# A list scheduler's rules re-tuned on a fused attention-and-MLP kernel: which step goes next, what is loaded first

## The chip, the cores and the metric

The kernel runs on one core of one Trainium2 chip. The metric is device time in microseconds of one execution, lower is better. The kernel before takes 282.93 us (median of 6 runs, 282.83 to 283.55). Ratios are computed from the mean time of one kernel's fast runs over the mean of the other's fast runs of the same rounds, so they are not quite the ratio of the medians that are quoted.

Engine names: PE is the matrix engine, DVE the vector engine, ACT the scalar engine, POOL the general one, SP the queue that issues all DMAs here.

## The reference, cut to what matters

x is 2048 tokens of 640 features in bf16. It is layer-normed once to xn, and two branches are added to it:

```python
def _A_ref(x, wqkv, w_phi, wo):        # 32 heads of 20
    q, k, v = split(x @ wqkv)
    pq, pk = q @ w_phi, k @ w_phi      # per head
    phi_q = concat(softmax(pq), softmax(-pq)); phi_k = concat(softmax(pk), softmax(-pk))
    kv = phi_k^T @ v;  z = sum over tokens of phi_k
    return (phi_q @ kv) / (phi_q @ z + 1e-6) merged @ wo
def _B_ref(x, w1, w3, w2):             # 1536 wide
    return (silu(x @ w1) * (x @ w3)) @ w2
xn = layernorm(x)
return x + _A_ref(xn, ...) + _B_ref(xn, ...)
```

Linear attention: the key side of all 2048 tokens has to be summed before the first query can be finished. The MLP has no such barrier, so its steps can fill holes in the attention branch.

## The kernel before

The program is not written in the order in which it runs. Eight generators ("streams") each offer their next step. A step is a short group of instructions. A loop asks every stream for its head, estimates with a cost table when that step could start, commits the best one to the instruction lists, and goes on. The result is a fixed list for every engine, and the engine works through it in that order: where PE's next matmul waits for a DMA, PE stands still (0.9 us before the fold in the profile below).

```python
streams = [norms(), attention(), k_norms(), loads(), fold_k(), o_transposes(), mlps(), outs()]
while any(alive):
    best = None
    for i in range(n):
        ...                                     # head of stream i, recorded as ops
        if any(o.eng == "PE" for o in ops):
            at = max(P.ready(ops), P.free["PE"] + 0.15)
        else:
            at = P.start_of(ops[0])
            if i == 2 and at < P.free["PE"] + 3.0:
                at -= 4.0                       # key sums early
            if i == 0 and at < P.free["PE"] + 2.0:
                at = -1.0                       # norms first of all
        if best is None or at < best[0]:
            best = (at, i, ops, after)
    ...
    P.commit(ops)

def first_loads():
    load_x(0, 1)
    load_x(1, 2)
    P.dma("SP", phi_s[:], phi_t)
    P.dma("SP", wv[:], wqkv_t[:, :, 2 * D:3 * D])
    load_x(2, 4)
    P.dma("SP", wqkT[:, DC:2 * DC, :], A_wqkv[:, D:2 * D], True)   # key weights, transposed by the DMA
    load_x(4, 8)
    w13(0, 512)                                                    # first third of w1 and w3, 1.31 MB
    load_x(8, 12)

def loads():                                    # cut: later transfers, after x tiles are normed
    for t in range(4, T):
        ...
        yield lambda t=t: P.dma("SP", xnT[:, :, t * 128:(t + 1) * 128], x_tok[:, t, :], True)
        if t == 7:
            yield lambda: (w13(512, 1024), load_x(12, 16))
        if t == 9:
            yield lambda: w13(1024, 1536)
            yield lambda: P.dma("SP", wqkT[:, 0:DC, :], A_wqkv[:, 0:D], True)   # query weights
```

The steps that the text speaks of: an *eviction* copies a result of PE out of its bank, by DVE or ACT, so that the bank is free again; the *warm-up* matmuls work on zeros before any data is there; a *value tile* or *key tile* is 10 matmuls of 320 columns for 128 tokens; the *fold* multiplies the transposed key weights (tile wqkT) with the block-diagonal of w_phi (tile BDc) into Wkp, which every key tile needs; a *q tile* is the last attention step of 128 tokens, with a chain of six DVE instructions behind it (the 1.5 us one writes prod); an *MLP step* is 10 matmuls of 512 columns and two DVE instructions (tiles t and hT); an *output tile* is 34 matmuls of 320 columns and one DVE add.

The softmax here doesn't subtract the row's maximum and nothing guards it: scores larger than these inputs give would overflow.

Of the kernel before, what the change touches and what calls it, by code (L numbers as in the profile page):

```python
# [9 lines left out]
D = 640  # L10
# [3 lines left out]
T = S // 128  # L14
# [228 lines left out]
def bass_parallel_sum__linear_kernel_hedgehog__glu_gated_swiglu__prompt_kernel(  # L243
# [13 lines left out]
    P = _Program(nc)  # L257
# [47 lines left out]
    wv = new("wv", [128, DC, D], bf, RKV + 6400)  # L305
# [87 lines left out]
    wqkv_t = A_wqkv.rearrange("(c p) n -> p c n", p=128)  # L393
# [4 lines left out]
    def w13(a, b):  # L398
        P.dma("SP", w1_s[:, :, a:b], w1_t[:, :, a:b])
        P.dma("SP", w3_s[:, :, a:b], w3_t[:, :, a:b])  # L400

    def load_x(a, b):
        P.dma("SP", x_tok[:, a:b, :], x_t[:, a:b, :])

    def first_loads():
        load_x(0, 1)
        load_x(1, 2)
        P.dma("SP", phi_s[:], phi_t)
        P.dma("SP", wv[:], wqkv_t[:, :, 2 * D:3 * D])
        load_x(2, 4)  # L410
        P.dma("SP", wqkT[:, DC:2 * DC, :], A_wqkv[:, D:2 * D], True)
        load_x(4, 8)
        w13(0, 512)
        load_x(8, 12)


# [29 lines left out]
    def ln_apply(t):  # L446
        o, m, s, z = x_tok[:, t, :], mv[:, t, 0:1], rstd[:, t, 0:1], rstd[:, t, 1:2]
        if t < 4 or P.free["DVE"] < P.free["ACT"]:
            P.op("DVE", "tensor_scalar", [o], [o, m, s], (o, o, m, s, ALU.subtract, ALU.mult),
                 cost=0.45)  # L450
        else:
            P.op("ACT", "activation", [o], [o, s, z], (o, o, ACT.Identity), dict(bias=z, scale=s),
                 cost=0.9)
# [138 lines left out]
    def load_xres(t):  # L592
        P.dma("SP", xres[:, t % 4, :], x_t[:, t, :])
# [30 lines left out]
    done = dict.fromkeys(("w", "ln", "t", "f", "k", "n", "kv", "q", "o", "h"), 0)  # L624

    def norms():
        yield lambda: (first_loads(), consts())
        for t in range(4):
            yield lambda t=t: ln_stats(t, 1)
            if t % 2:  # L630
                yield lambda t=t: ln_apply(t - 1)
                done["ln"] = t
                yield lambda t=t: ln_apply(t)
                done["ln"] = t + 1
            if t == 1:
                yield block_diag
        todo = []
        for t in range(4, T + 2, 2):
            if t == T or t > done["k"] + 6:
                for u in todo:  # L640
                    yield lambda u=u: ln_apply(u)
                    done["ln"] = u + 1
                todo = []
            if t == T:
                break
            while t > done["k"] + 6:
                yield None
            yield lambda t=t: ln_stats(t, 2)
            for u in todo:
                yield lambda u=u: ln_apply(u)  # L650
                done["ln"] = u + 1
            todo = [t, t + 1]
        yield consts_late

    def fold_k():
        for dc in range(DC):
            yield lambda dc=dc: fold_mm(1, dc, banks(2))
        done["f"] += 1
# [3 lines left out]
    def k_norms():  # L662
        for t in range(T):
            while done["k"] <= t:
                yield None
            yield lambda t=t: k_norm(t)
            done["n"] = t + 1

    def transposed(t):
        while done["ln"] <= t:  # L670
            yield None
        yield lambda: xn_transpose(t, banks(1))
        done["t"] = t + 1

    def loads():
        while done["t"] < 4:
            yield None
        for t in range(4, T):
            while done["ln"] <= t:
                yield None  # L680
            yield lambda t=t: P.dma("SP", xnT[:, :, t * 128:(t + 1) * 128], x_tok[:, t, :], True)
            done["t"] = t + 1
            if t == 7:
                yield lambda: (w13(512, 1024), load_x(12, 16))
                done["w"] = 8
            if t == 9:
                yield lambda: w13(1024, 1536)
                done["w"] = 12
                yield lambda: P.dma("SP", wqkT[:, 0:DC, :], A_wqkv[:, 0:D], True)
                done["f"] = 2  # L690

    def attention():
        def v(t):
            return lambda: v_tile(t, banks(2))

        yield lambda: warm_up(10, True)
        yield from transposed(0)
        yield lambda: warm_up(4, False)
        yield from transposed(1)
        yield v(0)  # L700
        yield v(1)
        yield from transposed(2)
        yield from transposed(3)
        yield v(2)
        yield v(3)
        while done["f"] < 1:
            yield None
        for t in range(T):
            while done["t"] <= t:
                yield None  # L710
            yield lambda t=t: k_tile(t, banks(2))
            done["k"] = t + 1
            if t >= 4:
                yield v(t)
            if 9 <= t < 14:
                while done["f"] < 2:
                    yield None
                yield lambda dc=t - 9: fold_mm(0, dc, banks(2))
        yield lambda: P.dma("SP", wo_s[:], A_wo.rearrange("(c p) d -> p c d", p=128))
        for fc in range(DC):  # L720
            yield lambda fc=fc: q_proj(0, fc, banks(1))
        while done["n"] < T:
            yield None
        for fc in range(DC):
            for sg in range(2):
                yield lambda fc=fc, sg=sg: kv_sum(sg, fc, banks(1))
        done["kv"] = 1
        yield lambda: P.dma("SP", w2_s[:], B_w2.rearrange("(c p) d -> p c d", p=128))
        yield lambda: (load_xres(0), load_xres(1))
        for b in range(NB):  # L730
            for j in range(4):
                t = 4 * b + j
                yield lambda t=t: q_tok(t, banks(4))
                done["q"] = t + 1
                if b + 1 < NB:
                    for fc in range((5 * j + 3) // 4, (5 * j + 8) // 4):
                        yield lambda b=b, fc=fc: q_proj(b + 1, fc, banks(1))

    def o_transposes():
        for t in range(T):  # L740
            while done["q"] <= t:
                yield None
            yield lambda t=t: P.dma("SP", oT[:, :, t * 128:(t + 1) * 128], o_tok[:, t % 3, :], True)
            done["o"] = t + 1

    def mlps():
        for b in range(NB):
            for fc in range(FC):
                while done["t"] < 4 * b + 4 or done["w"] <= fc or b == 2 and done["t"] < T or b == 3 and not done["kv"]:
                    yield None  # L750
                yield lambda b=b, fc=fc: mlp(b, fc, banks(2))
            done["h"] = b + 1

    def outs():
        for t in range(T):
            while done["o"] <= t or done["h"] <= t // 4:
                yield None
            yield lambda t=t: out_tile(t, banks(2))

    streams = [norms(), attention(), k_norms(), loads(), fold_k(), o_transposes(), mlps(), outs()]  # L760
    n = len(streams)
    heads, alive = [None] * n, [True] * n
    while any(alive):
        best = None
        for i in range(n):
            if heads[i] is None and alive[i]:
                s = next(streams[i], StopIteration)
                if s is StopIteration:
                    alive[i] = False
                else:  # L770
                    heads[i] = s
            if heads[i] is None:
                continue
            save = nmlp[0], len(finish)
            ops = P.step(heads[i])
            after = nmlp[0], finish[save[1]:]
            nmlp[0] = save[0]
            del finish[save[1]:]
            if any(o.eng == "PE" for o in ops):
                at = max(P.ready(ops), P.free["PE"] + 0.15)  # L780
            else:
                at = P.start_of(ops[0])
                if i == 2 and at < P.free["PE"] + 3.0:
                    at -= 4.0
                if i == 0 and at < P.free["PE"] + 2.0:
                    at = -1.0
            if best is None or at < best[0]:
                best = (at, i, ops, after)
        if best is None:
            continue  # L790
        at, i, ops, after = best
        nmlp[0] = after[0]
        finish.extend(after[1])
        P.commit(ops)
        heads[i] = None
# [61 lines left out]
```

## Time and profile before

| what | before |
|---|---|
| time, median of 6 | 282.93 us |
| span in the profile | 281.4 us |
| PE busy in it | 275.2 us (98%) |
| usual spacing of starts, 512 columns / 320 columns | 216 / 136 ns |
| sum of usual spacings over all 1890 matmuls | 271.7 us, 3.0 us of it warm-up |

The page of the kernel before: its first line of busy times, and three rows in which each digit is the busy share of one fortieth of the span in tenths (PEclk is the granted clock of PE).

```profile
PE 275.2 (98%) x1890; PEld 168.6 (60%) x1890; DVE 180.6 (64%) x317; ACT 108.6 (39%) x194; POOL 59.3 (21%) x90
...
PE   7799999999999999999999999999999999999996
...
DVE  4477988998464689989989999996631212121212
...
PEclk9999999999999999999999999999999999999999
```

PE is full almost everywhere, at full clock. What can still be won are small waits. The list of waits of PE (who waits, what ended the wait by the profile, us in total, times, longest; it counts no idle time under 150 ns):

```profile
PE PS L101 <- DVE t_68 L101: 1.6, 2, 1.3
PE PS L101 <- DMA wqkT<-in_A_wqkv_dram: 0.9, 1, 0.9
PE PS L101 <- DMA wv<-in_A_wqkv_dram: 0.5, 1, 0.5
PE PS L101 <- ACT Wkp L101: 0.5, 1, 0.5
```

The 1.3 us of the first line are the time before the first warm-up matmul. This list is not the whole loss. A matmul's end in the profile is its latency, not its turn on the array: the Trainium skill, "TensorE: Matmul & The Clock Gate", Single matmul latency, gives (398 + N) / 2.4 ns, that is 379 ns at 512 columns, and Back-to-back issue gap gives N / 2.4 + 2.5 for the gap of an isolated matmul, that is 216 ns; this trace has 379 ns, and 216 ns in unbroken streams. So a wait under 163 ns (379 - 216) leaves no idle time at all in the profile, and a longer one shows 163 ns too little. Below, "lost" is therefore the spacing between the starts of two neighbouring matmuls less the usual (median) spacing of that shape.

The timeline of PE in the kernel before, late in the attention stage (start, duration, what, idle before):

```profile
178.83 0.81 PE L101 MATMUL PS<-xnT,w_s 128*128 128x512 bf16 x3
179.72 0.86 PE L101 MATMUL PS<-KVc,EqT_81 128*128 128x154 bf16 x12
180.84 0.82 PE L101 MATMUL PS<-xnT,w_s 128*128 128x512 bf16 x3 [0.26 <-DVE t_68 L101]
```

Three 512-column matmuls need 0.65 us, and 0.89 us lie between the first two starts: 0.24 us lost, with no idle time listed (what is left of it, 0.08 us, is under 150 ns). Twelve q-tile matmuls need 0.69 us and took 1.12: 0.42 lost, where the profile lists 0.26. A third such place at 184.96 us costs 0.25 us. The busy table by stretches of the same kernel (window, its length, then busy us and instruction counts of PE, PE's weight loads, DVE, ACT, POOL; then clock, DMA share, GB/s) says why:

```profile
165.00:180.00 15.00, 14.92 (x95) 7.54 (x93) 14.30 (x27) 5.27 (x12) 0.00 (x0) 1.00 0.12 22
180.00:195.00 15.00, 14.65 (x76) 6.66 (x74) 13.32 (x23) 4.15 (x8) 0.00 (x0) 1.00 0.20 34
```

DVE is as full as PE there, and with q tiles and MLP steps alternating it falls behind.

The chain of waits of the kernel before (start, us, what), its start and one place of its later part:

```profile
3.33 8.43 DMA wqkT<-in_A_wqkv_dram
...
11.89 0.49 PE PS L101 x6
...
13.70 0.61 ACT Wkp L101
...
14.35 150.95 PE PS L101 x1062
...
178.17 1.50 DVE prod L101
...
180.11 0.69 DVE t_68 L101
```

At the start the transposed key weights (wqkT, landed at 11.76 us) and an eviction of the fold bound PE; from 165 to 185 us DVE pieces stand in the chain.

### The profile page before, as it was taken

To read this page: it belongs to the slowest core of one execution; us is meant where nothing else is said; L and a number is where in the kernel's file an instruction comes from. 1 tells how busy PE (TensorE), PEld (TensorE's weight loads), DVE (VectorE), ACT (ScalarE), POOL (GpSimd) and SP (SyncE) were. 2 spreads that over 40 slices of the span, in tenths; PEclk is the share of its full clock that TensorE was granted. 3 is DMA by queue.
4 is the path that set the end of the run, shared out by engine and by line. 5 is a ranking of instruction groups with operands and counts; after the bars stand their busy time and mean duration, and the time that the engine had idled before them with its cause. 6 is when DMAs were issued, how large, how long until landed. Compare 5 with 4: busy or idle time off the path is not lost.

```text
span 281.4 us, 4619 instructions
## 1 busy us (share of the span) xinstructions
PE 275.2 (98%) x1890; PEld 168.6 (60%) x1890; DVE 180.6 (64%) x317; ACT 108.6 (39%) x194; POOL 59.3 (21%) x90
## 2 busy tenths in 40 slices
PE   7799999999999999999999999999999999999996
PEld 2567765775469555555555555444467777777774
DVE  4477988998464689989989999996631212121212
ACT  3589888888510454474454533322200000000000
POOL 5443768799942000000000000000000000000000
PEclk9999999999999999999999999999999999999999
DMA  6987589720000772311121311320003131212211
GB/s 183 267 269 160 200 229 186 94 102 2 0 0 2 228 132 38 27 23 23 26 46 23 26 23 28 46 48 0 0 2 93 49 93 52 90 63 79 70 50 47
DMA packets 39654, 21.96 MB, mean 78 GB/s; under 512 B 26704, under 2 KB 39632, under 8 KB 39632
## 3 DMA queue, kind: packets, MB, share of 16 engines
q1 hardware_dynamic: 39632, 21.66, 31.9%
q8 instruction: 15, 0.25, 0.4%
q14 instruction: 7, 0.06, 0.1%
HBM read 12.81 MB, written 2.62 MB: 55 GB/s over the span
## 4 chain that ended last, share of the span: by engine, by line
PE 87%; DVE 6%; DMA 3%; issue 1%; SPq 1%; ACT 1%
PE PS L101 87%; DMA wqkT<-in_A_wqkv_dram 3%; DVE prod L101 2%; DVE t_68 L101 1%; SPq L113 1%; DVE den_s L101 1%; DVE hT_71 L101 1%; ACT Wkp L101 0%; DVE g_s L101 0%; DVE hT_79 L101 0%; DVE pr_s L101 0%; ACT xnT L101 0%; DVE xres L101 0%; ACT e_s L101 0%; DVE o_tok L101 0%
## 5 line engine op out<-in xcount | busy, mean ns | idle before, releaser
L101 PE MATMUL PS<-xnT,w_s 128*128 128x512 bf16 x480 | 107.2, 379 | 0.3 <-DVE t_68 L101 0.3
L101 PEld LDWEIGHTS PS<-xnT,w_s 128*128 128x128 bf16 x480 | 46.6, 98 | 55.7 <-DVE prod L101 0.6
L101 DVE TENSOR_TENSOR xres<-PS,xres 128x640 bf16<-128x640 f32 (+2 forms) x17 | 13.4, 785 | 60.0 <-PE PS L101 60.0
L101 ACT ACTIVATE th<-PS 128x512 f32<-128x512 f32 x48 | 28.7, 597 | 56.9 <-PE PS L101 56.9
L101 DVE SCALAR_TENSOR_TENSOR t_68<-th,PS 128x512 bf16<-128x512 f32 x48 | 32.8, 684 | 16.1 <-ACT th L101 16.1
L101 POOL TENSOR_TENSOR ekt<-ekt,rS_62 128x640 bf16<-128x640 bf16 x32 | 39.5, 1280 | 11.0 <-DVE rS_62 L101 11.0
L101 PE MATMUL PS<-wv,xnT 128*128 128x320 bf16 x160 | 24.0, 299 | 1.0 <-DMA wv<-in_A_wqkv_dram 0.5
L101 PE MATMUL PS<-wo_s,oT 128*128 128x320 bf16 (+2 forms) x160 | 24.5, 299 | 0.0
L101 DVE TENSOR_REDUCE S_61<-ekt 128x64 f32<-128x1280 bf16 x16 | 23.0, 1440 | 1.8 <-ACT ekt L101 1.8
L101 DVE TENSOR_TENSOR prod<-PS,g_s 128x1280 bf16<-128x1280 f32 x16 | 23.9, 1491 | 0.6
L101 PE MATMUL PS<-xnT,Wqp 128*128 128x512 bf16 x100 | 23.7, 379 | 0.0
L101 PE MATMUL PS<-Wkp,xnT 128*128 128x320 bf16 x160 | 23.7, 299 | 0.0
L101 ACT ACTIVATE ekt<-PS 128x640 bf16<-128x640 f32 x32 | 20.3, 707 | 4.4 <-PE PS L101 4.4
L101 PEld LDWEIGHTS PS<-wv,xnT 128*128 128x128 bf16 x160 | 15.5, 98 | 7.2 <-ACT Wkp L101 0.7
L101 PEld LDWEIGHTS PS<-wo_s,oT 128*128 128x128 bf16 x160 | 15.7, 98 | 6.3
L101 PEld LDWEIGHTS PS<-Wkp,xnT 128*128 128x128 bf16 x160 | 15.5, 98 | 6.0
L101 DVE BATCH_NORM_STATS2 bst<-x_tok 128x6 f32<-128x320 bf16 x32 | 15.1, 472 | 5.6 <-DMA x_tok<-in_A_x_dram 5.1
L101 PEld LDWEIGHTS PS<-xnT,Wqp 128*128 128x128 bf16 x100 | 9.4, 98 | 8.8
L101 ACT ACTIVATE e_s<-PS 128x64 f32<-128x64 f32 x32 | 9.0, 282 | 14.5 <-PE PS L101 13.5
L101 PE MATMUL PS<-w_s,hT_79 128*128 128x320 bf16 (+2 forms) x96 | 13.9, 299 | 0.0
L101 PE MATMUL PS<-w_s,hT_71 128*128 128x320 bf16 x96 | 13.7, 299 | 0.0
L101 PE MATMUL PS<-w_s,hT_76 128*128 128x320 bf16 x96 | 13.7, 299 | 0.0
(57 smaller groups left out, 267.3 us busy)
## 6 DMA issues: line engine op xcount, KB each, us to landing
w_s<-in_B_w_dram SPq DMA_DIRECT2D x6, 640.0 KB, 5.8
xres<-in_A_x_dram SPq DMA_DIRECT2D x16, 160.0 KB, 2.4
out_dram<-xres SPq DMA_DIRECT2D x15, 160.0 KB, 1.8
x_tok<-in_A_x_dram SPq DMA_DIRECT2D x3, 640.0 KB, 7.0
w_s<-in_B_w_dram SPq DMA_DIRECT2D x1, 1920.0 KB, 9.6
wv<-in_A_wqkv_dram SPq DMA_DIRECT2D x1, 800.0 KB, 5.8
wo_s<-in_A_wo_dram SPq DMA_DIRECT2D x1, 800.0 KB, 4.9
x_tok<-in_A_x_dram SPq DMA_DIRECT2D x2, 160.0 KB, 2.4
```

Of the source, the lines that this page charges most:

```text
L101: o = _Op(eng, lambda: m(*args, **kw), r, w, cost)
L113: o = _Op(eng, lambda: m(out, in_), self.regions(in_), self.regions(out), nbytes, True)
```

## The change

Intent: among steps that can start at the same time take the one of the lower rank, and put the MLP last while DVE is more than 4 us behind PE, so that something that needs no DVE goes first; let norms and key sums jump the line only when their data is there; and have MLP weights early so that MLP steps can fill holes. The diff, cut to its core:

```diff
     def first_loads():
         load_x(0, 1)
         load_x(1, 2)
+        load_x(2, 4)
+        P.dma("SP", wv[:], wqkv_t[:, :, 2 * D:3 * D])
+        w13(0, 512)
         P.dma("SP", phi_s[:], phi_t)
-        P.dma("SP", wv[:], wqkv_t[:, :, 2 * D:3 * D])
-        load_x(2, 4)
         P.dma("SP", wqkT[:, DC:2 * DC, :], A_wqkv[:, D:2 * D], True)
         load_x(4, 8)
-        w13(0, 512)
         load_x(8, 12)
@@ norms(): cut; tiles normed one by one, look-ahead limit 8 tiles in place of 6
@@ attention()
         yield v(0)
+        yield from transposed(2)
         yield v(1)
-        yield from transposed(2)
         yield from transposed(3)
@@ the loop
-    streams = [norms(), attention(), k_norms(), loads(), fold_k(), o_transposes(), mlps(), outs()]
+    MLPS, LAG = 6, 4.0
+    URGENT = {0: 4.0, 3: 4.0}
+    streams = [norms(), fold_k(), attention(), k_norms(), loads(), o_transposes(), mlps(), outs()]
+            rank = i
             if any(o.eng == "PE" for o in ops):
                 at = max(P.ready(ops), P.free["PE"] + 0.15)
+                if i == MLPS and P.free["DVE"] > P.free["PE"] + LAG:
+                    rank = n
             else:
                 at = P.start_of(ops[0])
-                if i == 2 and at < P.free["PE"] + 3.0:
-                    at -= 4.0
-                if i == 0 and at < P.free["PE"] + 2.0:
-                    at = -1.0
-            if best is None or at < best[0]:
-                best = (at, i, ops, after)
+                if i in URGENT:
+                    now, mine = P.free["PE"], P.free[ops[0].eng]
+                    if at <= max(now, mine) + 0.3 and at < now + URGENT[i]:
+                        at = now + 0.1 - URGENT[i]
+            if best is None or (round(at, 2), rank) < best[:2]:
+                best = (round(at, 2), rank, i, ops, after)
```

What it does to the instruction lists: no matmul and no byte is added or taken away. At the start PE does all four value tiles before the fold; late in the attention stage two output tiles stand between q tiles where MLP steps stood; a few evictions and norms change between DVE and ACT.

More of the change, by code (lines that the diff above doesn't have):

```diff
@@ L629, in norms @@
             yield lambda t=t: ln_stats(t, 1)
-            if t % 2:
+            if t:
                 yield lambda t=t: ln_apply(t - 1)
                 done["ln"] = t
-                yield lambda t=t: ln_apply(t)
-                done["ln"] = t + 1
-            if t == 1:
-                yield block_diag
+        yield lambda: ln_apply(3)
+        done["ln"] = 4
+        yield block_diag
         todo = []
         for t in range(4, T + 2, 2):
-            if t == T or t > done["k"] + 6:
+            if t == T or t > done["k"] + 8 or t == 12 and done["w"] < 8:
                 for u in todo:
@@ L645, in norms @@
                 break
-            while t > done["k"] + 6:
+            while t > done["k"] + 8 or t == 12 and done["w"] < 8:
                 yield None
@@ L778, in bass_parallel_sum__linear_kernel_hedgehog__glu_gated_swiglu__prompt_kernel @@
             del finish[save[1]:]
+            rank = i
             if any(o.eng == "PE" for o in ops):
                 at = max(P.ready(ops), P.free["PE"] + 0.15)
+                if i == MLPS and P.free["DVE"] > P.free["PE"] + LAG:
+                    rank = n
             else:
                 at = P.start_of(ops[0])
-                if i == 2 and at < P.free["PE"] + 3.0:
-                    at -= 4.0
-                if i == 0 and at < P.free["PE"] + 2.0:
-                    at = -1.0
-            if best is None or at < best[0]:
-                best = (at, i, ops, after)
+                if i in URGENT:
[4 more added lines that the diff above has]
+                best = (round(at, 2), rank, i, ops, after)
         if best is None:
             continue
-        at, i, ops, after = best
+        i, ops, after = best[2:]
         nmlp[0] = after[0]
```

## The prediction

> **What bounds the kernel.** PE. The page gives it 275.2 of 281.4 us busy (98%); the busy table by stretches has it full from 15 to 165 us and from 195 us to the last output tile, at a granted clock of 1.00. The timeline's spacing of starts (216 ns for a 512-column matmul, 136 ns for a 320-column one) sums over all 1890 matmuls to about 271.7 us, 3.0 us of it warm-up. PE's other waits are small: about 0.7 us before the first value tile (DMA of wv), 1.0 us before the first fold (wqkT, landed at 11.8 us), 0.65 us at a fold's eviction (ACT Wkp), and 0.9 us between 179 and 185 us, where q tiles and MLP alternate and DVE (13.3 to 14.3 of 15 us busy) is the slower. Some 3.3 us can be won at all, 1.2%; over 2% is out of reach.
>
> **What the change does.** Matmuls, bytes and sizes stay; some evictions and norm applies change engine. The instruction order shows:
> 1. Loads: x tiles 2-3 go ahead of wv, 1.31 MB of MLP weights ahead of phi and wqkT.
> 2. PE's start: four transposes and four value tiles come first, interleaved, then the key fold, unbroken; MLP fill only after four key tiles.
> 3. Norm statistics and key sums are re-ordered on DVE and ACT.
> 4. Late in the attention stage two output tiles stand between q tiles in place of MLP steps.
>
> **Cost, step by step.**
> - Wait for wv: stays (start 8.1 to 8.4 us). The second x transpose comes 0.3 us later, hidden behind wv. 0 to +0.2.
> - Value tiles: 40 x 136 ns plus two transposes of 0.3 us bring PE to the fold at about 14.3 us without a stall (in place of 1.0 + 0.65).
> - wqkT: the Trainium skill, "DMA: Bandwidth & Descriptors", Queues, rings and completion order, says that an engine consumes descriptors in ring order; this trace agrees, the 256-byte transpose packets run at full rate only once the 1280-byte ones are gone. 1.31 MB at the 355 GB/s at which these weights moved cost 3.7 us, less 0.5 to 1 us of bubble now filled: landing at 14.5 to 15.4. PE waits 0.2 to 1.1 us, say 0.6. Start in sum: -0.6 us.
> - 47 to 52 us: ACT gets four norm applies (0.92 us each) right before key-tile evictions (0.71 each) on which PE's banks hang. ACT then runs unbroken for some 10 us and PE, full before, should stall: estimate +0.7 us (0 to 1.3).
> - 165 to 185 us: an output tile needs of DVE one add (0.8 us) against 1.4 us for an MLP step, so DVE catches up: -0.9. The later, longer MLP run is PE-bound (2.16 us a step).
> - Tail unchanged.
>
> Sum: -0.8 us. Predicted 282.1 us, range 280.9 to 283.4. Chances: faster by over 2% 0.01, within 2% 0.97, slower 0.02.
>
> **What would show it.** Chain of waits: no DVE pieces around 165 to 185 us; wqkT lands near 15 us and is PE's largest wait at the start; PE below 100% near 50 us, released by ACT (eviction of ekt); PE busy in total about 275 us as before.
>
> **What would make it wrong.** wqkT after 16 us (MLP stands behind the fold in PE's order, so nothing fills: up to +2 us); no ACT stall at 50 us (then 281.3); a new stall where key tile 4 waits for its transposed x, or output tiles for oT.

## The result, and the profile after

The changed kernel took 282.49 us (median of 6, 282.31 to 283.56) against 282.93 us (6 runs): ratio 0.9987, 95% interval 0.9970 to 1.0004. By the 2% measure that is the same time, and 0.4 us less by the medians. The predicted 282.1 us with its range 280.9 to 283.4 holds it. Timed again on another occasion (5 rounds) it was 282.21 us against 282.82 us, ratio 0.9976, interval 0.9965 to 0.9988: a small gain, and this time clear of noise.

The page of the changed kernel, the same rows:

```profile
PE 274.5 (98%) x1890; PEld 168.4 (60%) x1890; DVE 182.7 (65%) x320; ACT 106.9 (38%) x191; POOL 59.1 (21%) x90
...
PE   7899999999999999999999999999999999999996
```

Its list of PE's waits:

```profile
PE PS L101 <- DVE t_68 L101: 1.3, 1, 1.3
PE PS L101 <- DMA wv<-in_A_wqkv_dram: 0.9, 1, 0.9
PE PS L101 <- DVE x_tok L101: 0.8, 2, 0.6
PE PS L101 <- DMA wqkT<-in_A_wqkv_dram: 0.6, 1, 0.6
```

The late wait for DVE is gone, the wait for the first weights has grown, and the fold still waits for its weights. The line with x_tok, the first two transposes waiting for their normed tiles, is hardly a loss: the first starts at 5.89 us against 5.86 before, and the second ends before the first weights land. The busy table of the changed kernel by the same stretches:

```profile
165.00:180.00 15.00, 15.00 (x121) 10.17 (x118) 13.01 (x25) 2.89 (x8) 0.00 (x0) 1.00 0.24 57
180.00:195.00 15.00, 15.00 (x81) 7.28 (x80) 11.73 (x20) 4.14 (x8) 0.00 (x0) 1.00 0.19 44
```

PE is full, and DVE has 1.3 to 1.6 us less to do in each stretch. The timeline of PE there shows one of the two output tiles (10 + 24 matmuls) between two q tiles; every start is at the usual spacing:

```profile
175.04 0.85 PE L101 MATMUL PS<-KVc,EqT_81 128*128 128x154 bf16 x12
175.73 1.52 PE L101 MATMUL PS<-wo_s,oT 128*128 128x320 bf16 x10
177.09 3.42 PE L101 MATMUL PS<-w_s,hT_76 128*128 128x320 bf16 x24
180.35 0.85 PE L101 MATMUL PS<-KVc,EqT_81 128*128 128x154 bf16 x12
```

The chain of waits of the changed kernel, from the key weights on:

```profile
5.47 9.93 DMA wqkT<-in_A_wqkv_dram
...
15.54 32.27 PE PS L101 x230
47.80 0.01 issue
47.82 0.48 PE PS L101 x6
48.29 0.07 issue
48.37 229.88 PE PS L101 x1580
```

But for the last add, no DVE piece is left in the later part. In front, the key weights now land at 5.47 + 9.93 = 15.40 us in place of 11.76, and PE starts the fold 0.14 us later. There are two small breaks near 48 us, which the kernel before did not have. The timeline of PE there:

```profile
46.99 0.81 PE L101 MATMUL PS<-xnT,w_s 128*128 128x512 bf16 x3
47.82 0.48 PE L101 MATMUL PS<-BDc,wqkT 128*128 128x140 bf16 x6
48.37 0.84 PE L101 MATMUL PS<-Wkp,xnT 128*128 128x320 bf16 x5
```

0.18 and 0.24 us are lost before the second and the third line, and the profile names nothing that ended these waits. The landing times do: the query weights landed at 47.68 us and the transposed x tile behind them at 48.23 us, each 0.14 us before the matmul that needs it, the same distance as at the fold.

Lost by PE, in us, by stretches of the span (spacing of starts less usual spacing; the first stretch begins with the first transpose):

| profile | first value tile starts at | fold starts at | 5.8 to 20 us | 45 to 56 us | 165 to 195 us |
|---|---|---|---|---|---|
| before | 8.13 | 11.89 | 2.54 | 0 | 0.95 |
| changed | 8.77 | 15.54 | 2.38 | 0.40 | 0 |
| changed, three more profiles (among the experiments) | 8.11 to 9.31 | 14.90 to 16.09 | 1.72 to 2.93 | 0.10 to 0.37 | 0 |

Everywhere else from 5.8 us to the end both lose under 0.1 us. In the first pair of profiles the last matmul ends at 278.91 us before and 278.24 us after, 0.7 us apart; the profiled executions took 283.25 and 282.45 us, so the one of before was 0.3 us on the slow side of its median.

### The profile page after: what moved, and what is told of

Read it like the earlier page. It is cut to its first block, busy times and chain, and to the rows that moved or that the text cites. A ratio compares the mean times of both kernels' runs of the same rounds, so it can differ in the third digit from the quotient of the medians.

```text
span 280.7 us, 4627 instructions
## 1 busy us (share of the span) xinstructions
PE 274.5 (98%) x1890; PEld 168.4 (60%) x1890; DVE 182.7 (65%) x320; ACT 106.9 (38%) x191; POOL 59.1 (21%) x90
## 4 chain that ended last, share of the span: by engine, by line
PE 94%; DMA 4%; SPq 2%; issue 0%; DVE 0%
PE PS L101 94%; DMA wqkT<-in_A_wqkv_dram 4%; SPq L113 2%; DVE xres L101 0%
## 5 line engine op out<-in xcount | busy, mean ns | idle before, releaser
L101 DVE SCALAR_TENSOR_TENSOR t_68<-th,PS 128x512 bf16<-128x512 f32 x48 | 32.8, 683 | 17.2 <-ACT th L101 17.2
L101 PEld LDWEIGHTS PS<-wo_s,oT 128*128 128x128 bf16 x160 | 15.6, 98 | 6.1
```

Source lines behind the costliest of these rows:

```text
L101: o = _Op(eng, lambda: m(*args, **kw), r, w, cost)
```

## The experiments

The chips of the three calls differ (the kernel before took 282.82 us in the first and 283.35 us in the second), so kernels of different calls are compared by their ratios. Where an edit below moves a load and keeps the plan, the run moved it in the finished queue; the diff shows where the load would stand in the source. In the first call the traces lack 18 of the 1890 matmul records; a missing record looks like 216 ns lost, and such places are left out of the sums.

### The changed kernel again

No edit.

> The changed kernel once more, unaltered, as a yardstick on this chip. Expected 0.4 to 0.5 us under the kernel before (ratio 0.998 to 0.999). In the trace: PE waits of about 0.9 us for wv, 0.6 to 0.8 us for wqkT near 15 us, 0.4 us near 48 us, none between 165 and 195 us.

Measured: 282.21 us (281.77 to 282.81) against 282.82 us (11 runs), ratio 0.9976. Lost: 2.93 us at the start, 0.19 us near 48 us, none late. wv landed at 9.17 us, half a microsecond later than in the first profile, with the same loads ahead of it. So the late gain repeats exactly, and the start does not: it moves with the landing of the first weights.

### Without the rule "MLP last"

```diff
-    MLPS, LAG = 6, 4.0
+    MLPS, LAG = 6, 1e9
```

> The changed kernel without its rule 'MLP last when DVE lags' (limit set out of reach); only the PE order between 165 us and the long MLP run changes back. Theory (the late stall of before went because output tiles let DVE catch up): PE loses about 0.9 us again between 165 and 195 us, released by DVE (prod, t), time 283.3 to 283.5, that is 0.4 to 0.5 us slower than before. Rival (the late stall went because the new scheduler shifted the streams against each other): no stall there, time 282.5 as the changed kernel.

Measured: 283.07 us (282.84 to 283.65), ratio to before 1.0011, interval 0.9999 to 1.0023. The busy table of this kernel:

```profile
165.00:180.00 15.00, 14.81 (x94) 7.62 (x94) 14.30 (x28) 5.02 (x12) 0.00 (x0) 1.00 0.12 22
180.00:195.00 15.00, 14.61 (x71) 6.46 (x70) 13.24 (x22) 4.13 (x8) 0.00 (x0) 1.00 0.20 34
```

DVE is back at 14.3 and 13.2 us, and the same three places lose 0.24, 0.42 and 0.25 us again, 0.94 in all, as in the kernel before. The time is 0.9 us above that of the changed kernel of the same rounds, a little under what was expected in absolute terms. The rival falls: without the rule nothing of the late gain is left, although the streams' new alignment is still there.

### The rule alone, on the kernel before

```diff
+            rank = i
             if any(o.eng == "PE" for o in ops):
+                if i == 6 and P.free["DVE"] > P.free["PE"] + 4.0:
+                    rank = n
                 at = max(P.ready(ops), P.free["PE"] + 0.15)
@@
-            if best is None or at < best[0]:
+            if best is None or (round(at, 2), rank) < best[:2]:
```

> The kernel before with only that one rule added; its first 165 us stay as they were. Theory: the 0.9 us between 165 and 195 us go, nothing else changes: 282.0 us, ratio 0.9965 to 0.997, which is 0.4 to 0.5 us better than the whole change, since the rest of the change then costs 0.3 us net. Rival (the rest of the change is worth something by itself): 282.5 or slower.

Measured: 281.95 us (281.40 to 282.59), ratio 0.9970, interval 0.9957 to 0.9982. The expectation hit. The late loss is gone (0), the start is that of the kernel before (fold at 11.77 us, 2.35 us lost). The edit brings the tie-break by rank along; the run above kept that and had the loss all the same, so it is the rule. By medians the one rule gives 0.9 us and the whole change 0.6 us in the same rounds; the two intervals overlap, so that the rest of the change costs something is likely by this pair, not shown by it.

### Query weights ahead of the last MLP weights

The order of every compute engine is kept, and so is the plan; only the place of one load in the DMA queue changes.

```diff
         if t == 9:
+            P.dma("SP", wqkT[:, 0:DC, :], A_wqkv[:, 0:D], True)
             w13(1024, 1536)
-            P.dma("SP", wqkT[:, 0:DC, :], A_wqkv[:, 0:D], True)
```

> The changed kernel with every instruction order kept but one: in the DMA queue the second transposed load (the query weights) goes ahead of the third load of MLP weights. Theory (the 0.4 us near 48 us are PE waiting for that load and for the transposed x tile queued behind it): wqkT lands about 4 us earlier, the 0.4 us go, 282.0 to 282.1 us. Rival (the prediction's: ACT's backlog of norm applies and key evictions holds the banks): the stall stays, with ACT as releaser, 282.4 to 282.5 us.

Measured: 282.50 us (281.79 to 284.22), ratio 0.9993, interval 0.9971 to 1.0015. The query weights landed at 42.5 us, 5 us earlier, and yet 0.81 us were lost, all at one place of the timeline of this kernel:

```profile
46.84 0.48 PE L101 MATMUL PS<-BDc,wqkT 128*128 128x140 bf16 x6
47.98 1.25 PE L101 MATMUL PS<-Wkp,xnT 128*128 128x320 bf16 x8 [0.66 <-ACT v L101]
```

The profile names ACT, but in the plan these matmuls need ACT only up to the key eviction before that one, which ended at 47.30 us. The transposed x tile landed at 47.85 us, and 47.98 is the same 0.13 to 0.14 us after. It stands behind the MLP weights in the queue, as before. The expectation failed, and it tells which byte mattered: moving one load ahead of another only changed which of two waits ended last. PE also came to this place earlier in this run (the fold began at 14.74 us), and the wait ate that.

### Last MLP weights behind all x tiles

```diff
-            w13(1024, 1536)            # at t == 9
...
+        w13(1024, 1536)                # behind the query weights and the last transposed x tile
```

> The changed kernel, every compute order kept; the third part of the MLP weights goes behind the query weights and behind all transposed x tiles in the DMA queue (their first use is after 80 us). The run with only the query weights moved kept the wait, now for the x tile. Theory (DMA queue alone): wqkT and the x tile land by 45 us and PE has no wait near 48 us: 0.4 us gained. The prediction's rival (ACT): in the trace of the changed kernel the eviction that frees the key tile's banks ends at 48.13 us, PE is free at 47.93, so 0.2 to 0.3 us remain, released by ACT. Time 281.9 to 282.3.

Measured: 281.86 us (281.50 to 283.40), ratio 0.9955, interval 0.9933 to 0.9978. The query weights landed at 43.42 us and the x tile at 44.03 us, well before their use. PE still lost 0.30 us, in the timeline of this kernel:

```profile
47.01 1.27 ACT L101 ACTIVATE ekt<-PS 128x640 bf16<-128x640 f32 x2
...
48.33 0.66 PEld L101 LDWEIGHTS PS<-Wkp,xnT 128*128 128x128 bf16 x6 [0.32 <-ACT ekt L101]
```

The key tile starts when ACT's eviction ends (48.28). So near 48 us there are two waits, one behind the other: DMA, which ends last in the changed kernel, and ACT, which held PE for 0.3 us by itself here. The prediction named only the second. The theory of the DMA alone falls as much as the prediction's. In time the move's own gain is not shown: the interval overlaps that of the changed kernel (0.9965 to 0.9988).

### First MLP weights back behind the key weights

Again the plan and all compute orders of the changed kernel are kept.

```diff
         P.dma("SP", wv[:], ...)
-        w13(0, 512)
         P.dma("SP", phi_s[:], phi_t)
         P.dma("SP", wqkT[:, DC:2 * DC, :], ..., True)
         load_x(4, 8)
+        w13(0, 512)
         load_x(8, 12)
```

> The changed kernel, every compute order kept; in the DMA queue alone the first MLP weights (1.31 MB) go back behind the key weights and x tiles 4-7, where they were before. Theory (the load order costs the new plan its start): wqkT lands near 12 us in place of 15 to 16, PE reaches the fold at 14.6 and goes through with at most 0.2 us of eviction wait; the wait for wv (1.1 us) stays; 0.8 us faster than the changed kernel, 281.4 to 281.8, unless the wait near 48 us takes some of it back. Rival (the order of loads is as the change intends, MLP weights are wanted early): PE stalls for w1 or w3 at the first MLP step near 22 us, no gain or a loss.

Measured: 280.96 us (280.54 to 282.38) against 283.35 us for the kernel before in these rounds, ratio 0.9928, interval 0.9907 to 0.9949. wqkT landed at 10.81 us, PE entered the fold at 13.81 us without a wait, and no MLP step waited for its weights. The timeline of PE there:

```profile
11.10 2.88 PE L101 MATMUL PS<-wv,xnT 128*128 128x320 bf16 x20
13.81 1.89 PE L101 MATMUL PS<-BDc,wqkT 128*128 128x140 bf16 x30
```

Lost at the start: 0.68 us, near 48 us still 0.17. The interval lies below that of the changed kernel (0.9965 to 0.9988). The gain is larger than expected; in the profiled execution (280.54 us) the early landing of wv (7.69 us) is a part of that, for the median it is not shown. The intended benefit of early MLP weights does not exist in this plan: their first use came at 21.0 us in this run, and they had landed by 17.2 us.

### Both moves

> Both moves in the DMA queue together on the changed kernel's plan. Theory: they add, PE's waits after 5.8 us shrink to 1.1 us for wv and at most 0.4 us in all the rest: about 1.1 us under the changed kernel, 281.0 to 281.4 us, ratio 0.9935 to 0.995 to before, the fastest of all; rival: one hides in the other and the sum is under 0.8 us.

The edit is the two diffs above together. Measured: 280.87 us (280.65 to 280.98), ratio 0.9912, interval 0.9897 to 0.9928: the fastest median, and the narrowest spread. Its chain of waits:

```profile
2.20 5.98 DMA wv<-in_A_wqkv_dram
8.18 0.14 issue
8.32 268.34 PE PS L101 x1866
```

From the first value tile to the end PE waits for nothing of weight (1.15 us lost between 5.8 and 20 us, 0.95 of it before the first value tile; 0.01 us near 48 us, and 0.16 and 0.09 in two more profiles below). Against the single move of the first weights the intervals overlap, so that the second move adds anything to the time is not shown.

### The new load order under the old plan

```diff
 # kernel before, every engine's order kept; first loads only
-x 0, x 1, phi, wv, x 2-3, wqkT, x 4-7, w13(0, 512), x 8-11
+x 0, x 1, x 2-3, wv, w13(0, 512), phi, wqkT, x 4-7, x 8-11
```

> The kernel before, its plan of every engine kept, only its first loads in the order of the changed kernel (x 2-3, wv, MLP weights, phi, key weights). Theory: wqkT lands at 15.0 to 16.0, and since the fold stands right after two value tiles in this plan, PE waits for it from about 11.4 us: 3.5 to 4 us in place of 1.0, time 285.8 to 286.7. That is what the new order of PE's start hides. Rival (load order is worth little either way): within 1 us of before.

Measured: 288.14 us (287.32 to 288.62), ratio 1.0167, interval 1.0146 to 1.0188. The direction is right and the size is not: 1.4 us more than the top of the expectation. wqkT landed at 15.49 us, as expected. The busy table of this kernel, three windows around the wait for the fold (it begins at 11.4 us and ends at 15.63 us):

```profile
14.00:15.50 1.50, 0.00 (x0) 0.00 (x0) 0.00 (x0) 0.00 (x0) 1.42 (x4) 1.00 1.08 199
15.50:18.50 3.00, 2.87 (x29) 2.90 (x30) 1.36 (x3) 2.07 (x4) 0.89 (x3) 0.50 1.00 354
18.50:20.00 1.50, 1.50 (x16) 1.23 (x14) 1.40 (x5) 1.50 (x3) 0.00 (x0) 0.86 0.42 138
```

The third number from the right is the granted clock: it is 0.50 for 3 us after the wait. The Trainium skill, "TensorE: Matmul & The Clock Gate", HAM oscillation, gives the rule as "no PE-idle gaps >~3.4µs"; here a gap of 3.9 us (4.1 us lost) had this effect, and the matmuls from 15.6 to 20 us lost 1.55 us to it. The sum then closes: the first value tile starts 0.7 us later (wv), 3.0 more for wqkT, 1.55 of clock, 0.65 less for an eviction that is now hidden, together 4.6, and the last matmul ends 4.64 us later than in the kernel before. None of the other kernels has such a gap.

### Four more looks at the landing of wv

No edit: two profiles of "both moves", two of the changed kernel.

> One more profile of both moves, for the landing of wv, the term of the prediction that was sized wrong. So far wv landed at 7.77 to 9.17 us (mean 8.54) in six profiles with the MLP weights right behind it and at 7.69 and 8.18 us in two without them, both kinds with x tiles 2-3 ahead of it; 8.00 and 7.85 us in the two with the old order. Theory (the weights behind it slow its last packets): 7.6 to 8.2 us here, and 8.3 to 9.2 us in the looks at the changed kernel. Rival (x tiles 2-3 ahead of it, or chance): no difference between the two kinds.

> One more profile of the changed kernel, for the landing of wv: 8.3 to 9.2 us by the theory that the weights behind it slow it, 7.7 to 8.2 us as often as not by the rival.

> A second look of the kind without the MLP weights behind wv: theory 7.6 to 8.2 us; rival, anywhere in 7.7 to 9.2 us.

> A second look of the kind with the MLP weights right behind wv: theory 8.3 to 9.2 us; rival, anywhere in 7.7 to 9.2 us.

Measured: wv landed at 8.63 and 8.48 us with both moves, at 8.28 and 7.98 us in the changed kernel. That is the reverse of the theory, which falls. Over all profiles with x tiles 2-3 ahead of wv: 7.77 to 9.17 us in eight with the MLP weights right behind it (mean 8.44), 7.69 to 8.63 us in four without (mean 8.25). The landing of the first large load simply varies by up to 1.5 us between executions. With the old order it was 8.00 and 7.85 us in two profiles; whether x tiles 2-3 ahead of wv cost a few tenths stays open.

## Why the prediction was right

Point by point, against the sum that it rested on (-0.6 + 0.7 - 0.9 = -0.8 us; measured -0.44 and -0.6 us in time, -0.7 in the first pair of profiles: -0.16 at the start, +0.40, -0.95). The late term was right; the two others were off in size, the start by 0.3 to 0.4 and the place near 48 us by 0.3 or more the other way. That these two nearly cancel is luck.

- **PE bounds the kernel, and only about 3.3 us can be won.** Right. The best variant found is 2.5 us (0.9%) under the kernel before of its rounds.
- **165 to 185 us: -0.9.** Right in size and in cause. 0.95 us before, 0 in every kernel with the rule, 0.94 again without it; the rule alone on the kernel before gives the gain by itself. Output tiles have one DVE instruction for 4.6 us of PE work (34 x 136 ns), so DVE catches up.
- **Start: -0.6.** Right in sign at most. The step "Wait for wv: stays ... 0 to +0.2" is the term that was mis-sized: the first value tile began at 8.77 us instead of 8.13 in the first profile (+0.64), and between 8.11 and 9.31 us in three more. The rest of the step held: PE went through four value tiles without a stall, reached the fold about 14.75 us (14.3 predicted, the difference is wv), and wqkT landed at 15.40 us, at the upper end of "14.5 to 15.4". Lost at the start: 2.38 us against 2.54, and 2.26 as the mean of four profiles, so -0.2 to -0.3 in place of -0.6. Nor do the prediction's own terms give -0.6: 0.6 for wqkT in place of 1.0 + 0.65, and 0 to 0.2 for wv, would be about -0.95. "PE's largest wait at the start" was wqkT (about 0.8 us lost in each of the four profiles) in two of them and wv in the other two (1.10 and 1.58).
- **47 to 52 us: +0.7, by ACT.** The place was right, the size (0.40 us; 0.10 to 0.40 over four profiles) lies in the stated 0 to 1.3, the named cause was the second of two waits. In all four profiles of the changed kernel the wait that ends last there is a DMA (in the first the query weights at 47.68 us and an x tile at 48.23 us; ACT's eviction ended at 48.13): two thirds of the MLP weights, the query weights and the x tile stood close together in one queue (the two thirds issued 5.8 us apart, 12.1 before; DMA share 1.09 between 30 and 45 us against 0.78 before). That is the new plan's doing and not that of the late x tiles 4-7 (landed at 18.0 us against 14.3): with the first MLP weights back they landed at 13.40 us, the thirds were still 5.9 us apart, and the x tile still held PE for 0.17 us (landed 46.31, matmul 46.44). With that queue cleared, 0.01 to 0.30 us of ACT's wait remain (four profiles). The reading failed because the prediction looked at ACT's backlog and not at the queue for the same stretch.

What the change as a whole shows: one of its parts, the rule for MLP steps, is worth about 0.9 us. The new load order delays the key weights by 3.6 us, and the new order on PE (four value tiles first) hides most of that delay; under the old order of PE the same loads cost 4.6 us in the trace and 1.7% in time. Put the loads back and keep the new order, and the kernel is 280.9 to 281.0 us, in rounds in which the kernel before took 283.35. The expected gain of the change was thus partly spent on feeding MLP weights that nothing used for another 10 us.

Not settled: what makes wv land anywhere between 7.7 and 9.2 us, and with it how much of the 0.2 us between the two comparisons of the changed kernel (-0.44, -0.61 us) is chance.

## What to carry to other kernels

In a program whose order is fixed ahead, judge a load by when its first user stands in the order, not by how useful it might be: here 1.31 MB of weights went ahead of the key weights that PE needed first, and these landed 3.6 us later. When the scheduler has a choice of filler, choose by the engine that is behind: an output tile that hardly needs DVE is worth more than an MLP step while DVE lags. And undo each part of a mixed change alone; the whole hid a gain of 0.9 us late, some 0.2 gained at the start where about 1.3 was to be had (with the loads put back, 0.68 to 1.59 us were lost there in four profiles, 2.54 before), and 0.1 to 0.4 lost near 48 us.

## What the Trainium skill lacked or had wrong

- "DMA: Bandwidth & Descriptors", Queues, rings and completion order: the page has an engine consume descriptors in ring order, and the traces agree (the key weights landed 3.64 us later with 1.31 MB ahead of them, 0.36 MB per us; moving the MLP weights brought them back to 10.8 to 11.8 us). The page says nothing of how far the landing of the same early load varies: 7.69 to 9.17 us for 0.8 MB in twelve profiles with the same loads ahead of it.
- No page that was read gives the time from a DMA's landing to the start of the matmul that waits for it: 0.13 to 0.14 us in every case here (15.40 to 15.54, 47.68 to 47.82, 48.23 to 48.37, 8.18 to 8.32). It served to name what ended a wait where the profile named nothing or named ACT.
- "DMA: Bandwidth & Descriptors" has no figure for an issuing queue that is held up: the small phi load's issue took 0.43 us before and 1.58 us behind the MLP weights, the transposed key weights 6.39 and 7.87 us; x tiles 4-7 behind them were issued at 13.39 us in place of 9.77.
- "TensorE: Matmul & The Clock Gate" was right in 379 and 216 ns at 512 columns, and in half the clock after a gap over about 3.4 us (here for about 3 us, after 3.9 us). But Back-to-back issue gap calls the 216 ns that of an isolated matmul and gives about 131 ns as the sustained spacing at 512 columns; none of the 594 spacings after such a matmul was under 215 ns in the kernel before. The page does not say what latency and spacing mean for a list of waits: 0.95 us lost showed as 0.3 us of waiting.
